# One written order of issue for every engine of a long-convolution, modulation and sparse-expert block

## The chip, the cores and the metric

The kernel runs on one core of a Trainium2 chip. The metric is the device time of the whole program in microseconds (us), as a median of several executions. The engines are TensorE (PE; PEld is its weight load), VectorE (DVE), ScalarE (ACT), GpSimd (POOL) and SyncE (SP, which here only issues DMAs). Each works through its own queue in order.

## The reference, cut to what matters

The input has 2048 tokens of 640 channels. Six modulation vectors come from c and w_mod. Part A is a long convolution over the tokens, written with FFTs; part B picks eight tokens and runs a gated MLP on them.

```python
sa, ca, ga, sb, cb, gb = (silu(c) @ w_mod) in six parts
h = layernorm(x) * (1 + ca) + sa                 # x = A_q
kv = (four-tap causal convolution of A_k) * A_v
y = irfft(rfft(pad(kv)) * rfft(pad(A_ssm_k)))[:2048] + kv * A_ssm_D
x = x + ga * (h * y)
h = layernorm(x) * (1 + cb) + sb
r = h @ w_r;  idx = the 8 tokens with the largest r
out_B = (silu(h[idx] @ w_gate) * (h[idx] @ w_up)) @ w_down * sigmoid(r[idx])
x = x + gb * (h + scatter_add(idx, out_B))
```

## The kernel before

The 640 channels are five blocks (0 to 4) of 128. Tokens are 16 groups m of 128. For each block the filter (gA) and the product kv (xA) are Fourier-transformed in two matmul stages, multiplied, and transformed back in two.

- load_kv brings k and v of a block in transposed, by DMA transposes on SP. conv applies the four taps as matmuls with diagonal matrices (make_diag), VectorE multiplies by v, and kvT goes to DRAM through POOL's queue; load_xA reads it back in another layout.
- stage_A multiplies 16 slices by the table RA, four to a PSUM tile, and each of the four tiles is evacuated into A. stage_B multiplies A by the table FT: eight PSUM tiles of 1024 columns into HX. The tables come from iotas and Sin.
- product makes the complex product on VectorE, in six operations of 1024 elements for each half of a block, with three temporaries.
- stage_BT is the first inverse stage (table IT), four tiles into U, stored to DRAM (Ud) by POOL; load_uA reads it back. stage_AT finishes the inverse (table RAT), multiplies by h, adds into xq, takes the statistics of the second layer norm (bn_stats, L398) and transposes xq to get the router's sums.
- In between stand the modulation (load_wmod, modulation), and the first layer norm: statistics (L471), then h in 16 operations (L479) and four pairs of 2560 wide ones (L483, L484).
- Tail: the statistics are aggregated (bn_aggr), xn is normalised, the eight tokens are selected by small VectorE operations and matmuls, xn is gathered by one-hot matmuls, three projections follow (L657, L677), then for every group six matmuls with the identity add up gb*sb, xq and xn*gb*(1+cb) (L693 to L695), ScalarE copies (L696), SP stores, and POOL scatter-adds the eight rows (L701).

All PSUM tiles of two banks come from one ring of four. A helper (Balance.copy, L44 and L46) gives each evacuation to ScalarE or, in a set share (0.4, then 0.2, then 0.125), to VectorE; a line L44 or L46 in the profile is that helper. The order of SP and POOL is the order of the program text; TensorE, ScalarE and VectorE are ordered by the framework's scheduler.

Of the kernel before, what the change touches and what calls it, by code (L numbers as in the profile page):

```python
# [9 lines left out]
P = 128  # L10
# [9 lines left out]
NB = 5  # L20
# [11 lines left out]
class Balance:  # L32


    def __init__(self, nc):
        self.nc = nc
        self.share = 0.0
        self.acc = 0.0

    def copy(self, out, in_):  # L40
        self.acc += self.share
        if self.acc >= 1.0 - 1e-9:
            self.acc -= 1.0
            self.nc.vector.tensor_copy(out=out, in_=in_)  # L44
        else:
            self.nc.scalar.copy(out=out, in_=in_)  # L46


def _kernel_body(ctx, tc, A_q, A_k, A_v, A_shift_k, A_ssm_k, A_ssm_D,
# [3 lines left out]
    ctx.enter_context(tc.manual_schedule(engines={mybir.EngineType.SP, mybir.EngineType.Pool}))  # L53
    bal = Balance(nc)
# [22 lines left out]
    kTs, vTs, gAs = [], [], []  # L77

    def load_kv(b):
        kT = ring.tile([P, 16 + S_TOK], BF, name="kT", tag="K")  # L80
        vT = ring.tile([P, S_TOK], BF, name="vT", tag="K")
# [3 lines left out]
        kTs.append(kT)  # L85
        vTs.append(vT)
# [16 lines left out]
    trig = big.tile([P, 4, 1024], F32, name="trig", tag="HX", bufs=3)  # L103
# [20 lines left out]
    load_kv(0)
    with nc.allow_non_contiguous_dma(reason="tiny transposed loads"):
        nc.scalar.dma_start(out=shk_bf[:], in_=A_shift_k.rearrange("(b p) j -> p b j", p=P))
        load_g(0, nc.scalar)
        Dt_rows = bass.AP(tensor=Dt[:].tensor, offset=Dt[:].offset, ap=[[16 * Dt[:].ap[0][0], 8], [1, NB * M]])
        D_rows = bass.AP(tensor=A_ssm_D.tensor, offset=A_ssm_D.offset, ap=[[1, 8], [8, NB * M]])
        nc.scalar.dma_start(out=Dt_rows, in_=D_rows)  # L130
        load_g(1, nc.scalar)
        nc.scalar.dma_start(out=cT_bf[:], in_=c.rearrange("o (t p) -> p (o t)", p=P))
        nc.scalar.dma_start(out=wr_c[:], in_=B_w_r.rearrange("(t p) -> p t", p=P))
    load_kv(1)
    V_ph = trig[:, 0:2, :]
    for hf in range(2):
        iota(trig[:, hf, :].rearrange("p (a b) -> p a b", a=8), [[4, 8], [64, P]], base=32 * hf + 1)
    nc.gpsimd.memset(halfpi[:], math.pi / 2)
    iota(irow[:], [[1, P]])
    nc.gpsimd.memset(onesb[:], 1.0)  # L140


    shk_f = const.tile([P, NB, 4], F32, name="shk_f")

    def make_diag(b):
        if b == 0:
            V.tensor_copy(out=shk_f[:], in_=shk_bf[:])
        for j in range(4):
            V.tensor_scalar(out=diag[:, b, j, :], in0=ident[:], scalar1=shk_f[:, b, j:j + 1], scalar2=None,
                            op0=ALU.mult)  # L150

    def diag_b(b):
        return diag[:, b]

    ecol = const.tile([P, 1], F32, name="ecol")
    V.tensor_scalar(out=ecol[:], in0=pidx[:], scalar1=-7.5, scalar2=1.0 / 16, op0=ALU.add, op1=ALU.mult)
    V.tensor_scalar(out=ecol[:], in0=ecol[:], scalar1=MAGIC, scalar2=None, op0=ALU.add)
    V.tensor_scalar(out=ecol[:], in0=ecol[:], scalar1=-MAGIC, scalar2=None, op0=ALU.add)
    mcol = const.tile([P, 1], F32, name="mcol")
# [36 lines left out]
    IT = const.tile([P, M, 3, P], BF, name="IT")

    def make_table(hf):
        k0 = 8 * hf
        if hf == 0:  # L200
            V.tensor_scalar(out=pc[:], in0=pidx[:], scalar1=1.0 / 8192, scalar2=None, op0=ALU.mult)
        ph, qq, ab = trig[:, hf, :], trig[:, 2, :], trig[:, 3, :]
        V.tensor_scalar(out=qq, in0=ph, scalar1=pc[:], scalar2=MAGIC, op0=ALU.mult, op1=ALU.add)
        V.tensor_scalar(out=qq, in0=qq, scalar1=-MAGIC, scalar2=None, op0=ALU.add)
        V.scalar_tensor_tensor(out=ph, in0=ph, scalar=pc[:], in1=qq, op0=ALU.mult, op1=ALU.subtract)
        fl = lambda s: FT[:, s, k0:k0 + 8, :].rearrange("p a b -> p (a b)")
        nc.scalar.activation(out=fl(1), in_=ph, func=ACT.Sin, scale=TWO_PI)
        nc.scalar.activation(out=fl(2), in_=ph, func=ACT.Sin, scale=-TWO_PI)
        V.scalar_tensor_tensor(out=ab, in0=ph, scalar=-1.0, in1=ph, op0=ALU.mult, op1=ALU.max)
        nc.scalar.activation(out=fl(0), in_=ab, func=ACT.Sin, scale=-TWO_PI, bias=halfpi[:])  # L210

    short_tables(0)
    make_diag(0)
    make_table(0)
    make_table(1)

    def make_inverse_table():
        for s, d in ((0, 1), (1, 2), (2, 0)):
# [3 lines left out]
            bal.copy(IT[:, :, d, :], pt[:])  # L222


    def stage_A(src, A, u):
        for g4 in range(4):
# [5 lines left out]
            bal.copy(o, ps[:])  # L232

    def stage_B(A, HX):
        for kk in range(8):
            ps = ps_tile([P, 2, 512])
            for i in range(2):
                k2 = 2 * kk + i
                f = lambda a: a.rearrange("p kc u d -> p (kc u d)")
# [6 lines left out]
            bal.copy(HX[:, 2 * kk:2 * kk + 2].rearrange("p k c u d -> p (k c u d)"),  # L246
                     ps[:].rearrange("p a b -> p (a b)"))

    T3 = {}

    def product(xt, ux, ht, uh):
        if "a" not in T3:
            T3["a"] = ring.tile([P, 2, 8, P], BF, name="Ta", tag="V", bufs=2)
            T3["b"] = ring.tile([P, 8, P], BF, name="Tb", tag="V", bufs=2)
        t0, t1, t2 = T3["a"][:, 0], T3["a"][:, 1], T3["b"][:]
        for hk in range(2):
            ks = slice(8 * hk, 8 * hk + 8)
            Xr, Xi = xt[:, ks, 0, ux, :], xt[:, ks, 1, ux, :]
            Hr, Hi = ht[:, ks, 0, uh, :], ht[:, ks, 1, uh, :]
# [501 lines left out]
```

## Time and profile before

| | us |
|---|---|
| median of 3 runs (range) | 274.51 (273.98 to 276.78) |
| the profiled execution's own time | 272.93 |
| its span, first to last instruction | 271.1 |
| busy: PE, DVE, ACT, POOL | 164.4, 182.0, 114.3, 15.5 |
| mean granted clock of TensorE (1 is 2.4 GHz) | 0.81 |

The profile is one execution. A busy time is the sum of an engine's instructions, which can overlap by some 0.08 us on VectorE; the chain of work gives what one instruction adds. Idle time of an engine that isn't late costs nothing.

### The profile page before, as it was taken

To read this page: it belongs to the slowest core of one execution; us is meant where nothing else is said; L and a number is where in the kernel's file an instruction comes from. 1 tells how busy PE (TensorE), PEld (TensorE's weight loads), DVE (VectorE), ACT (ScalarE), POOL (GpSimd) and SP (SyncE) were. 2 spreads that over 40 slices of the span, in tenths; PEclk is the share of its full clock that TensorE was granted. 3 is DMA by queue.
4 is the path that set the end of the run, shared out by engine and by line. 5 is a ranking of instruction groups with operands and counts; after the bars stand their busy time and mean duration, and the time that the engine had idled before them with its cause. 6 is when DMAs were issued, how large, how long until landed. Compare 5 with 4: busy or idle time off the path is not lost.

```text
span 271.1 us, 3680 instructions
## 1 busy us (share of the span) xinstructions
PE 164.4 (61%) x1428; PEld 116.6 (43%) x1428; DVE 182.0 (67%) x443; ACT 114.3 (42%) x124; POOL 15.5 (6%) x40
## 2 busy tenths in 40 slices
PE   0039969999998705650693879386455410489950
PEld 0025546557665504420372648265355400375730
DVE  5159965762477999999969219977867899502300
ACT  0149356344868703600671789135310115002850
POOL 5000200000000010000000000002100000000002
PEclk9999997999999965786588699959955755558995
DMA  8960999999999210500004400534889770000450
GB/s 152 237 76 4 245 239 243 361 378 256 251 347 244 100 77 4 155 0 0 0 9 180 123 0 7 217 92 165 299 265 392 232 248 1 2 2 0 154 210 28
DMA packets 67897, 40.64 MB, mean 150 GB/s; under 512 B 44768, under 2 KB 64680, under 8 KB 67880
## 3 DMA queue, kind: packets, MB, share of 16 engines
q1 hardware_dynamic: 58944, 31.48, 43.1%
q0 software_dynamic: 2192, 7.88, 7.6%
q10 hardware_dynamic: 6744, 1.06, 2.6%
q8 instruction: 11, 0.18, 0.3%
q14 instruction: 6, 0.05, 0.1%
HBM read 24.67 MB, written 10.50 MB: 130 GB/s over the span
## 4 chain that ended last, share of the span: by engine, by line
PE 38%; DVE 34%; DMA 10%; issue 10%; ACT 3%; POOL 1%; POOLq 1%; SPq 0%; DVEq 0%; ACTq 0%
PE ps L389 4%; DVE st L471 4%; PE ps L240 4%; PE ps L229 4%; DMA kvd<-kvT 4%; DMA gA<-in_A_ssm_k_dram 3%; DVE t L394 3%; PE ps L349 3%; PE ps L307 3%; DMA xq<-in_A_q_dram 2%; PE ps L277 2%; PE ps L677 2%; PE ps L279 2%; DVE xq L396 2%; DVE h L479 2%
## 5 line engine op out<-in xcount | busy, mean ns | idle before, releaser
L240 PE MATMUL ps<-A,FT 128*128 128x512 bf16 x80 | 33.1, 414 | 18.8 <-ACT HX L46 12.7
L46 ACT CAST HX<-ps 128x1024 bf16<-128x1024 f32 x31 | 29.9, 1023 | 32.2 <-DVE HX L263 16.9
L46 ACT CAST A<-ps 128x1024 bf16<-128x1024 f32 x30 | 28.3, 1028 | 17.9 <-PE ps L229 17.9
L229 PE MATMUL ps<-RA,gA 128*128 128x256 bf16 x80 | 14.1, 349 | 21.4 <-DVE gA L324 21.1
L242 PE MATMUL ps<-A,FT 128*128 128x256 bf16 x80 | 23.4, 293 | 0.0
L244 PE MATMUL ps<-A,FT 128*128 128x256 bf16 x80 | 23.4, 293 | 0.0
L46 ACT COPY xT<-ps 128x2048 bf16<-128x2048 bf16 x4 | 7.5, 1866 | 34.8 <-PE ps L401 34.8
L277 PE MATMUL ps<-IT,HX 128*128 128x256 bf16 x80 | 19.8, 289 | 2.5 <-DVE HX L264 2.3
L46 ACT CAST U<-ps 128x1024 bf16<-128x1024 f32 x18 | 17.4, 1020 | 8.6 <-PE ps L279 8.0
L229 PEld LDWEIGHTS <-gA 128*128 128x128 bf16 x80 | 9.7, 124 | 24.8 <-DVE gA L324 21.4
L279 PE MATMUL ps<-IT,HX 128*128 128x256 bf16 x80 | 19.4, 289 | 0.5 <-DVE HX L265 0.5
L44 DVE CAST A<-ps 128x1024 bf16<-128x1024 f32 x10 | 12.1, 1222 | 10.9 <-PE ps L229 10.9
L307 PE MATMUL ps<-kT,early 128*128 128x512 bf16 x80 | 18.1, 379 | 0.4 <-ACT A L46 0.4
L242 PEld LDWEIGHTS <-FT 128*128 128x128 bf16 x80 | 8.4, 105 | 20.1 <-issue 18.4
L394 DVE TENSOR_TENSOR t<-ps,h 128x1024 bf16<-128x1024 f32 x10 | 12.0, 1222 | 6.5 <-PE ps L389 4.0
L398 DVE BATCH_NORM_STATS2 st<-xq 128x6 f32<-128x128 bf16 x80 | 16.0, 280 | 0.1
L471 DVE BATCH_NORM_STATS2 st<-xq 128x6 f32<-128x320 bf16 x32 | 13.6, 465 | 3.3 <-DMA xq<-in_A_q_dram 3.3
L401 PE MATMUL ps<-ident,xq 128*128 128x128 bf16 x80 | 6.5, 245 | 15.2 <-DVE xq L396 15.2
L696 ACT CAST xq<-ps 128x640 bf16<-128x640 f32 x16 | 11.1, 692 | 11.0 <-PE ps L695 10.1
L309 DVE TENSOR_TENSOR kvT<-ps,vT 128x1024 bf16<-128x1024 f32 x10 | 12.2, 1222 | 4.0 <-PE ps L307 3.8
L229 PE MATMUL ps<-RA,xA 128*128 128x256 bf16 x80 | 13.2, 331 | 0.6 <-ACT A L46 0.5
L244 PEld LDWEIGHTS <-FT 128*128 128x128 bf16 x80 | 8.4, 105 | 11.2 <-issue 3.0
(189 smaller groups left out, 337.0 us busy)
## 6 DMA issues: line engine op xcount, KB each, us to landing
Ud<-U POOLq DMA_DIRECT2D x10, 512.0 KB, 2.9
uA<-Ud SPq DMA_DIRECT2D x10, 512.0 KB, 4.0
kvd<-kvT POOLq DMA_DIRECT2D x5, 512.0 KB, 5.1
xA<-kvd SPq DMA_DIRECT2D x5, 512.0 KB, 5.1
xq<-in_A_q_dram SPq DMA_DIRECT2D x4, 640.0 KB, 7.7
out_dram<-xq SPq DMA_DIRECT2D x4, 640.0 KB, 3.2
wg<-in_B_w_gate_dram SPq DMA_DIRECT2D x1, 2160.0 KB, 11.7
wu<-in_B_w_up_dram SPq DMA_DIRECT2D x1, 2160.0 KB, 16.4
```

The costliest lines, as they stand in the source:

```text
L46: self.nc.scalar.copy(out=out, in_=in_)
L229: nc.tensor.matmul(ps[:, bb // 2, :, (bb % 2) * 8:(bb % 2) * 8 + 8], lhsT=src[:, 4 * g4 + bb, :], rhs=RA[:].rearrange("p k c e -> p (k c) ...
L240: nc.tensor.matmul(ps[:, i, :], lhsT=FT[:, 0, k2, :], rhs=f(A[:, 2 * k2:2 * k2 + 2]), start=True, stop=False)
L242: nc.tensor.matmul(ps[:, i, 0:256], lhsT=FT[:, 1, k2, :], rhs=f(A[:, 2 * k2 + 1:2 * k2 + 2]), start=False, stop=False)
L244: nc.tensor.matmul(ps[:, i, 256:512], lhsT=FT[:, 2, k2, :], rhs=f(A[:, 2 * k2:2 * k2 + 1]), start=False, stop=True)
L277: nc.tensor.matmul(ps[:, i, :], lhsT=xt[:, k2, 0, ux, :], rhs=IT[:, k2, 1:3, :].rearrange("p a b -> p (a b)"), start=True, stop=False)
L279: nc.tensor.matmul(ps[:, i, :], lhsT=xt[:, k2, 1, ux, :], rhs=IT[:, k2, 0:2, :].rearrange("p a b -> p (a b)"), start=False, stop=True)
L307: nc.tensor.matmul(ps[:, i, :], lhsT=diag_b(b)[:, j, :], rhs=kT[:, n0 - j:n0 - j + 512], start=(j == 0), stop=(j == 3))
L309: V.tensor_tensor(out=kvT[:, 1024 * i2:1024 * i2 + 1024], in0=ps[:].rearrange("p a b -> p (a b)"), in1=vT[:, 1024 * i2:1024 * i2 + 1024], ...
L394: V.tensor_tensor(out=t[:].rearrange("p m (g j) -> p m g j", g=2), in0=ps[:].rearrange("p g m j -> p m g j"), in1=h[:, :, cc].rearrange("p ...
L398: V.bn_stats(out=st2[:, m, b, :], in_=xq[:, m, c0:c0 + P])
L471: V.bn_stats(out=st[:, m, hf, :], in_=xq[:, m, hf * 320:hf * 320 + 320])
```

## The change

Every queue gets its order from one text. The stages become generators that stop after each piece (an evacuation, a half of a product, four groups of statistics), and a string ORDER names the pieces in the order in which all engines get them; a star sends an evacuation to VectorE, the others go to ScalarE. The functions keep their contents but for these points:

- The product works in place in HX, in two operations of 2048 (filter broadcast over the real and imaginary rows) and two of 1024 per half; filter and kv of one block now share one HX, and HX has two buffers in place of three.
- The diagonals of blocks 1 to 4 and the constants of the selection are made on POOL; the absolute value of the table is made on ScalarE; kv is stored by SP from a single kvT buffer; the first loads come in another order, and the tiny loads of D move to SP.
- bn_aggr is replaced by eight short operations over all groups (moments).
- In the tail the PSUM ring is released and split. Two matmul pairs per group add gb*sb and xq ("base", two PSUM tiles), in portions put before the gather, between the projections, before and after the last one; VectorE then multiplies and adds xn ("finish"), and SP stores xn.

```diff
+ORDER = """
+START RA DIAG0 DIAG2 TAB0 LK2 RA TAB0:2 C0:2 LK1 G0 TAB1:3 DIAG1 G0* C2:2 G0 LXA0 G0* RAT:2 C1 LW:4 IT DIAG3
+IT IT* C1 MOD LG2 X0* X0 X0* X0 MOD LW:2 B0* B0 B0* B0 P0 B0:4 LG1 P0:2 MOD:4 OG LXA1 G1:3 G2 P0 COL LX G1
+X1:2 BT0 X1 Sx G2 Sx:8 BT0 LK3 C3 X1 BT0:2 LXA2 B1:4 Sx:2 G2:2 LG3 B1 Sx:5 X2 LK4 Sx C3 X2:2 LG4 X2 B1:2 P1
+H:2 B1 B2:3 G3 P1:2 DIAG4 C4 G3 B2 H B2 G3 P1 G3 LXA3 X3 H:3 B2:3 C4 LXA4 H:3 X3:3 BT1:3 H BT1 B3:5 LU0 H G4
+B3 P2 G4 B3 H B3 P2:2 AT0 X4 AT0 G4:2 BT2:2 LU1 WG P2 P3 X4:2 S0 P3 X4 BT2 AT1 BT2 B4:2 P3 LU2 B4:3 P3 P4 B4:3
+BT3:2 S0 P4:2 S0 BT3:2 LU3 P4 AT1 S0 S1 BT4 S1:2 BT4:3 S1 R0 AT2:2 R0 R1 S2:3 AT3:2 R1 S2 S3:2 R2 LU4 AT4 R2
+R3 AT4 R3 R4 WG S3:2 S4:4 R4 WD TC
+"""
-    ctx.enter_context(tc.manual_schedule(engines={mybir.EngineType.SP, mybir.EngineType.Pool}))
+    ctx.enter_context(tc.manual_schedule())
...
+            (V if b == 0 else nc.gpsimd).tensor_scalar(out=dg[:, j, :], in0=ident[:], scalar1=shk_f[:, b, j:j + 1],
...
+        kvT = ring.tile([P, S_TOK], BF, name="kvT", tag="V")
...
+        nc.sync.dma_start(out=kvds[b][:], in_=kvT[:])
...
-            V.tensor_tensor(out=t0, in0=Xr, in1=Hr, op=ALU.mult)
-            V.tensor_tensor(out=t1, in0=Xi, in1=Hi, op=ALU.mult)
-            V.tensor_tensor(out=t2, in0=Xr, in1=Hi, op=ALU.mult)
-            V.tensor_tensor(out=Xi, in0=Xi, in1=Hr, op=ALU.mult)
-            V.tensor_tensor(out=Xr, in0=t0, in1=t1, op=ALU.subtract)
-            V.tensor_tensor(out=Xi, in0=Xi, in1=t2, op=ALU.add)
+            X = hx[:, ks, :, 1, :]
+            Xr, Xi = hx[:, ks, 0, 1, :], hx[:, ks, 1, 1, :]
+            Hr, Hi = (hx[:, ks, i:i + 1, 0, :].to_broadcast([P, 8, 2, P]) for i in range(2))
+            V.tensor_tensor(out=T2[:], in0=X, in1=Hi, op=ALU.mult)
+            V.tensor_tensor(out=X, in0=X, in1=Hr, op=ALU.mult)
+            yield
+            V.tensor_tensor(out=Xr, in0=Xr, in1=T2[:, :, 1, :], op=ALU.subtract)
+            V.tensor_tensor(out=Xi, in0=Xi, in1=T2[:, :, 0, :], op=ALU.add)
+            yield
...
+    def t_S1():
         for m in range(M):
+            for hf in range(2):
+                V.bn_stats(out=st1[:, m, hf, :], in_=xq[:, m, hf * 320:hf * 320 + 320])
+            yield
+        mu1, var1 = moments(st1[:], 4, 160, "a")
...
+    def base(ms):
+        for m in ms:
+            po = back.tile([P, 2, 512], F32, name="po", tag="o", bufs=2)
+            for hf in range(2):
+                cc = slice(hf * 320, hf * 320 + 320)
+                nc.tensor.matmul(po[:, hf, 0:320], lhsT=ident[:], rhs=gbs[:, cc], start=True, stop=False)
+                nc.tensor.matmul(po[:, hf, 0:320], lhsT=ident[:], rhs=xq[:, m, cc], start=False, stop=True)
+            nc.scalar.copy(out=xq[:, m, :].rearrange("p (h d) -> p h d", h=2), in_=po[:, :, 0:320])
...
+    norm(rest[4:])
+    base(range(0, 4))
...
+    def finish(ms, store=None):
+        for m2 in ms:
+            x2 = xn[m2 // 4][:, 2 * (m2 % 4):2 * (m2 % 4) + 2, :]
+            V.tensor_tensor(out=x2, in0=x2, in1=gbo[:, None, :].to_broadcast([P, 2, D]), op=ALU.mult)
+            V.tensor_tensor(out=x2, in0=x2, in1=xq[:, 2 * m2:2 * m2 + 2, :], op=ALU.add)
+            if m2 % 2 == 1:
+                nc.sync.dma_start(out=out_d[:, 2 * m2 - 2:2 * m2 + 2, :],
+                                  in_=xn[m2 // 4][:, 2 * (m2 % 4) - 2:2 * (m2 % 4) + 2, :])
...
     pg = proj(wg)
...
+    base(range(4, 8))
     pu = proj(wu)
...
+    finish(range(0, 2))
+    hT = small.tile([P, NFC, NSEL], BF, name="hT")
+    V.tensor_tensor(out=hT[:], in0=gs[:], in1=pu[:], op=ALU.mult)
+    base(range(8, 10))
...
+    base(range(10, 16))
+    finish(range(2, 4))
```

The names in ORDER: C convolution halves, G and X stage_A for filter and kv, B stage_B, P product, BT and AT the inverse stages, S statistics and R router sums of a block, Sx and H the first layer norm, MOD, OG, COL modulation, TAB, RA, RAT, IT tables, LK, LG, LXA, LU, LW, LX, WG, WD loads of k and v, filter, kv, inverse data, w_mod, x and the expert weights, TC the selection's constants. "P0:2" is two pieces of block 0's product. Rings that held four buffers (K for k, v, U, t and xT; G for gA, xA and uA) get five and six.

## Rows read from the trace of the kernel before

**Rows 1.** Windows: busy us (instructions) per engine, granted clock, DMA share, GB/s.
```profile
18.00:36.00 18.00, 17.23 (x98) 10.39 (x99) 17.84 (x42) 13.46 (x14) 1.57 (x4) 1.00 0.56 126
36.00:69.00 33.00, 29.89 (x191) 19.25 (x190) 17.71 (x23) 15.77 (x19) 1.18 (x3) 0.95 1.09 293
69.00:90.00 21.00, 18.63 (x158) 13.19 (x157) 14.88 (x25) 16.75 (x17) 0.53 (x1) 1.00 1.02 268
90.00:105.00 15.00, 3.40 (x32) 2.45 (x29) 15.00 (x58) 3.51 (x4) 1.28 (x3) 0.72 0.17 70
105.00:131.00 26.00, 11.54 (x58) 7.52 (x59) 25.66 (x47) 7.25 (x8) 0.00 (x0) 0.70 0.14 41
158.00:183.00 25.00, 19.11 (x173) 14.83 (x173) 18.38 (x39) 13.44 (x14) 1.06 (x2) 0.86 0.26 86
248.20:262.00 13.80, 13.18 (x97) 9.28 (x96) 4.17 (x5) 10.96 (x16) 0.00 (x0) 1.00 0.41 144
```

**Rows 2.** Waits: who waited for whom, us in total, times, longest.
```profile
ACT HX L46 <- DVE HX L263: 16.9, 1, 16.9
```

**Rows 3.** Chain that ended last, middle of the kernel: start us, us, what.
```profile
57.24 3.46 PE ps L307 x16
...
87.67 0.60 DVE Ta L260
...
94.64 0.75 DVE st L471 x2
...
111.55 5.70 DVE h L479 x16
117.25 2.80 DVE h L483 x2
...
143.22 2.35 DVE t L394 x2
...
208.84 3.45 PE ps L389 x32
```

**Rows 4.** The same chain, the tail.
```profile
214.78 3.19 DVE st L398 x16
...
223.50 3.92 DVE xn L591 x11
...
237.70 3.89 PE ps L657 x140
...
242.01 6.22 PE ps L677 x28
...
262.13 3.24 DMA out_dram<-xq
```

**Rows 5.** Timeline of ScalarE near 70 us: start us, us, engine, line, operation.
```profile
69.82 5.59 ACT L46 CAST A<-ps 128x1024 bf16<-128x1024 f32 x6 [0.24 <-PE ps L229]
```

**Rows 6.** Timeline of the first 5 us, POOL and VectorE.
```profile
1.82 0.29 POOL masks.py:199 TENSOR_SCALAR_AFFINE_SELECT ident<-ident 128x128 bf16<-128x128 bf16 x1
...
2.26 1.99 POOL L117 IOTA trig<- 128x1024 f32 x2
...
3.47 0.86 DVE L157 TENSOR_SCALAR ecol<-ecol 128x1 f32<-128x1 f32 x1
...
4.39 0.15 DVE L158 TENSOR_SCALAR ecol<-ecol 128x1 f32<-128x1 f32 x1
```

**Rows 7.** Timeline of SP, which issues transposes and loads.
```profile
25.70 1.24 SPq L83 DMA_TRANSPOSE kT<-in_A_k_dram  x1
...
55.93 10.73 SPq L83 DMA_TRANSPOSE kT<-in_A_k_dram  x1
```

**Rows 8.** DMA issues: count, KB each, median us to landing.
```profile
xA<-kvd SPq DMA_DIRECT2D x5, 512.0 KB, 5.1
xq<-in_A_q_dram SPq DMA_DIRECT2D x4, 640.0 KB, 7.7
...
early<-in_w_mod_dram SPq DMA_DIRECT2D x2, 800.0 KB, 7.5
```

More of the change, by code (lines that the diff above doesn't have):

```diff
@@ L231, in stage_A, with t_G, t_X, t_C @@
             o = A[:, :, u, g4 * 32:g4 * 32 + 32].rearrange("p kc (g j) -> p g kc j", g=2)
-            bal.copy(o, ps[:])
-    def stage_B(A, HX):
+            evac(o, ps[:])
+            yield
+    def t_G(b):
+        V.tensor_tensor(out=gAs[b][:, :, 0], in0=gAs[b][:, :, 0], in1=Dt[:, b * M:(b + 1) * M], op=ALU.add)
+        yield from stage_A(gAs[b], b, 0)
+    def t_X(b):
+        yield from stage_A(xAs[b], b, 1)
+    def t_C(b):
+        kT, vT = kTs[b], vTs[b]
+        kvT = ring.tile([P, S_TOK], BF, name="kvT", tag="V")
+        for i2 in range(2):
+            ps = ps_tile([P, 2, 512])
+            for i in range(2):
+                n0 = 16 + 512 * (2 * i2 + i)
+                for j in range(4):
+                    nc.tensor.matmul(ps[:, i, :], lhsT=diags[b][:, j, :], rhs=kT[:, n0 - j:n0 - j + 512],
+                                     start=(j == 0), stop=(j == 3))
+            V.tensor_tensor(out=kvT[:, 1024 * i2:1024 * i2 + 1024], in0=ps[:].rearrange("p a b -> p (a b)"),
+                            in1=vT[:, 1024 * i2:1024 * i2 + 1024], op=ALU.mult)
+            if i2 == 0:
+                yield
+        kvds[b] = dram.tile([P, S_TOK], BF, name="kvd%d" % b)
+        nc.sync.dma_start(out=kvds[b][:], in_=kvT[:])
+        yield
+    def t_B(b):
+        A = As[b]
+        HX = HXs[b] = big.tile([P, M, 2, 2, P], BF, name="HX", tag="HX", bufs=2)
+        f = lambda a: a.rearrange("p kc u d -> p (kc u d)")
         for kk in range(8):
@@ L315, in _kernel_body @@
[L315 to L329 removed]
+        yield
+    h_ = {}
+    rsum = small.tile([P, M, 2], F32, name="rsum")
@@ new lines, in t_S, with t_R @@
+    def t_S(b):
+        if b == 0:
+            h_["st2"] = small.tile([P, M, NB, 6], F32, name="st2", tag="st")
+        st2 = h_["st2"]
+        for m in range(M):
+            V.bn_stats(out=st2[:, m, b, :], in_=xq[:, m, b * P:(b + 1) * P])
+            if m % 4 == 3:
+                yield
+    def t_R(b):
+        pt = ps_tile([P, M, P], BF)
+        for m in range(M):
+            nc.tensor.transpose(pt[:, m, :], xq[:, m, b * P:(b + 1) * P], ident[:])
+        xT = ring.tile([P, M, P], BF, name="xT", tag="K", bufs=5)
+        evac(xT[:], pt[:])
+        yield
+        pr = ps_tile([P, M, 2])
+        for m in range(M):
+            nc.tensor.matmul(pr[:, m, :], lhsT=xT[:, m, :], rhs=wcol[:, b, :], start=True, stop=True)
+        if b == 0:
+            V.tensor_copy(out=rsum[:], in_=pr[:, :, :])
+        else:
+            V.tensor_tensor(out=rsum[:], in0=rsum[:], in1=pr[:, :, :], op=ALU.add)
+        yield
@@ L459, in _kernel_body @@
-    bal.share = 0.125
-    product(X1, 1, X0, 0)
-    stage_B(A2, X2)
-    stage_BT(X1, 1, 0)
-    load_uA(0)
-    og, sg = modv[:, 1, :], modv[:, 0, :]
-    V.tensor_tensor(out=og, in0=og, in1=modv[:, 2, :], op=ALU.mult)
-    V.tensor_tensor(out=sg, in0=sg, in1=modv[:, 2, :], op=ALU.mult)
-    st = small.tile([P, M, 2, 6], F32, name="st1", tag="st")
-    mv1 = small.tile([P, M, 2], F32, name="mv1")
-    for m in range(M):
-        for hf in range(2):
-            V.bn_stats(out=st[:, m, hf, :], in_=xq[:, m, hf * 320:hf * 320 + 320])
-        V.bn_aggr(out=mv1[:, m, :], in_=st[:, m, :, :])
@@ new lines, in _kernel_body, with once, run @@
+    tasks = {}
+    def once(f, b):
+        f(b)
+        yield
+    def run(name, n):
+        kind = name.rstrip("0123456789")
+        if name not in tasks:
+            arg = name[len(kind):]
+            tasks[name] = MAKERS[kind](*([int(arg)] if arg else []))
+        for _ in range(n):
+            next(tasks[name])
+    MAKERS = dict(START=t_START, TC=t_TC, RA=lambda: short_tables(0), RAT=lambda: short_tables(2), DIAG=t_DIAG,
+                  TAB=t_TAB, IT=t_IT, G=t_G, X=t_X, C=t_C, B=t_B, P=t_P, BT=t_BT, LU=t_LU, AT=t_AT, S=t_S, R=t_R,
+                  LW=t_LW, MOD=t_MOD, OG=t_OG, COL=t_COL, LX=t_LX, Sx=t_S1, H=t_H, WG=t_WG, WD=t_WD,
+                  LK=lambda b: once(load_kv, b), LG=lambda b: once(load_g, b), LXA=lambda b: once(load_xA, b))
@@ new lines, in _kernel_body, with pm_tile @@
+    for item in ORDER.split():
+        name, _, n = item.partition(":")
+        evac.vector = name.endswith("*")
+        run(name.rstrip("*"), int(n) if n else 1)
+    for name, t in tasks.items():
+        assert next(t, "end") == "end", name
+    front.close()
+    back = ctx.enter_context(tc.tile_pool(name="back", bufs=1, space=bass.MemoryType.PSUM))
+    wg, wu, wd = W["g"], W["u"], W["d"]
+    def pm_tile(shape, dtype=F32):
+        return back.tile(list(shape), dtype, name="pm", tag="m", bufs=2)
@@ L594, in _kernel_body, with norm @@
-    prT = ps_tile([M, P], BF)
+    xn = [big.tile([P, 8, D], BF, name="xn", tag="HX", bufs=2) for _ in range(2)]
+    on_act = NORM_ON_SCALAR
+    def norm(ms):
+        for m in ms:
+            o, i_ = xn[m // 8][:, m % 8, :], xq[:, m, :]
+            if m in on_act:
+                nc.scalar.activation(out=o, in_=i_, func=ACT.Identity, scale=rs2[:, m:m + 1], bias=nm2[:, m:m + 1])
+            else:
+                V.tensor_scalar(out=o, in0=i_, scalar1=rs2[:, m:m + 1], scalar2=nm2[:, m:m + 1], op0=ALU.mult,
+                                op1=ALU.add)
@@ L595, in _kernel_body @@
+    rest = [m for m in range(M) if m not in on_act]
+    norm(on_act)
+    prT = pm_tile([M, P], BF)
     nc.tensor.transpose(prT[:, :], r_bf[:], ident[:])
+    norm(rest[0:1])
     rT = small.tile([M, P], F32, name="rT")
```

626 lines of the change are left out of this document (265 added, 361 removed).

## Prediction

> **What bounds the kernel now.** I read the windows first. From 36 to 90 us TensorE is busy about nine tenths of the time and the DMA is saturated, at 268 to 293 GB/s [rows 1]. From 90 to 131 us VectorE alone is full (15.0 of 15 us, 25.7 of 26), while TensorE works 3.4 and 11.5 us and ScalarE 3.5 and 7.3 [rows 1]. The list of waits says why: ScalarE once waited 16.9 us to write HX until VectorE had read the old HX in the product [rows 2]; that product stood in VectorE's queue behind the layer norm's statistics (0.75 us a token group) and all of h (5.70 us, then four pairs of about 2.80) [rows 3]. So no engine bounds this kernel: long runs on one engine's queue starve the others. From 131 us on the engines take turns as well (19.1 and 18.4 of 25 us) [rows 1]. At the end lies a serial tail: after the last statistics (214.78 + 3.19 = 217.97 us) [rows 4] come selection, experts, the 96 combining matmuls, the store and the scatter-add, 53.1 us to the span's end.
>
> **Unit costs.** 16 matmuls of 512 columns take 3.46 us, 0.42 us per 1000 columns; 32 of 128 took 3.45 us late in the kernel, 0.84 per 1000, which is the 1.2 GHz level [rows 3]. VectorE takes 0.60 us for a bf16 operation 1024 wide and 1.40 for 2560, so 0.07 + 0.52 per 1000 elements; from PSUM 1024 cost 1.17 (2.35 for two) [rows 3]. ScalarE evacuates 1024 in 0.93 us when it doesn't wait (5.59 for six) [rows 5].
>
> **Product.** A half of a block was six operations of 1024, 3.60 us; it becomes two of 2048 (1.13 each, by the line above) and two of 1024: 3.46. The elements are the same, so ten halves save 1.4 us in all. [...]
>
> **Moves between engines.** Seven evacuations stay on VectorE (the starred names in ORDER) and ScalarE takes the others, at 0.93 us where VectorE pays 1.17. VectorE also loses 16 diagonals, two absolute values and the bn_aggr. The moves count in the stage sums below. The 16 diagonals and the eight table operations go to POOL, and this isn't free: a one-element VectorE operation that takes 0.15 us took 0.86 beside POOL's iotas, and ended as these did (2.26 + 1.99 = 4.25 us) [rows 6]. A POOL operation of 128x128 is 0.29 us [rows 6], so 24 of them can hold VectorE 0 to 7 us, more if they are slower than that row; I take 2, since they are spread and VectorE gives some up anyway. [...]
>
> **Stage A, up to block 3's first convolution half.** The matmul head starts earlier: the first Sin no longer stands behind a wait for c. But the DMA decides this stage. SP's order puts block 3's transposes behind all of w_mod and x, and a transpose issued onto a full queue held SP 10.73 us [rows 7]. Before, the queue paused until block 2's load went out at 25.70 [rows 7]; now that load follows block 0's at once, so I let the queue run on from 18 us, when the first four transposes are through. After that it must move four transposes, three kv stores, two kv loads and two filter blocks (11 x 512 KB), six of w_mod (800 KB) and four of x (640 KB) [rows 8]: 13.0 thousand KB or 13.3 MB, at 293 to 268 GB/s 45.4 to 49.6 us. So block 3's v lands at 63 to 68 us; I take 66. The stores of kv move from POOL's queue to SP's, behind transposes, and kvT has one buffer, so VectorE waits in its queue for each store, with layer norm and product behind it; this costs nothing in the sum, as VectorE, by the same count of pieces as in stage B, has some 41 us of work in these 66. If that cover is gone it costs up to 5 us for each of three stores (a transfer of that size in [rows 8]).
>
> **Stage B, the rest of ORDER's line 3 to the end of line 7.** I count each line's pieces and take the fullest engine. Line 3: 16 evacuations, ScalarE 14.9 us (VectorE 12.9). Line 4: 27 evacuations, 25.1 (VectorE 22.9, TensorE 22.8). Line 5: VectorE 23.6 (nine product pieces of P2, P3 and P4's first are 16.1, three inverse halves AT at 1.17 + 0.60 make 5.3, h 1.4, statistics 0.8). Line 6: VectorE 26.5 (P4 4.7, six AT halves 10.6, 13 quarter blocks of statistics at 0.80 = 10.4, rest 0.8). Line 7: VectorE 6.9. Sum 97.0 us; VectorE alone has 92.8, TensorE 75 by its columns at 2.4 GHz. Nothing runs without waits across a four-deep PSUM ring: the fullest engine reached 0.91, 0.89 and 0.76 in three mixed stretches, and 0.99 where one engine starved the others [rows 1]. I take 0.90: 107.8 us, with 97 to 129 as ends. What is late next is ScalarE in line 4, VectorE in 5 and 6.
>
> **Tail.** Four products of 1280 leave the selection's chain (0.73 each by the unit cost, 2.9), one of 11 normalisations moves to ScalarE (0.36, a share of 3.92 [rows 4]), and eight short operations replace the 16 aggregations that stand between 217.97 and the first normalisation at 223.50 [rows 4] (5.5 us with the inverse root; I take 0.5 of it, at most 2): -3.8 us. The 16 matmuls (5120 columns) now between the two projections delay the second by up to 4.3 us at 1.2 GHz, the level that this stretch had (6.22 us for 28 x 320 columns [rows 4]). Then hT stands on VectorE behind the sigmoid, which waits for ScalarE's copies, and four operations of 0.73: 3.5 us against 1.95 for a projection (half of 3.89 [rows 4]): +1.6. After the experts' last matmul the old tail took 13.9 us to the last copy (248.23 to 262.13 [rows 4]; 96 matmuls at 2.4 GHz [rows 1]); now 24 matmuls and six copies (0.69 each, 10.96 for 16 [rows 1]) run beside VectorE's delta (640 from PSUM, about 0.8 by the 1.17 for 1024) and eight operations of 0.73, 6.6 together: -7.3. The store (3.24 us [rows 4]) and the scatter behind it stay. Sum -5.2: 47.9 us; 44 if the interleaved matmuls lift the clock to 2.4 GHz before the experts, 51 if the delta waits.
>
> **Sum.** 66 + 107.8 + 2 + 47.9 = 223.7 us of span. The profiled execution of before lay 1.8 us above its span and 1.6 below the median: 227.1 us.
>
> **Rivals.** *Ring-bound:* fixed orders make the engines wait for each other as in the stretch at 0.76 [rows 1]; stage B takes 129 us, the kernel 248. For it: four PSUM slots as before, and no queue can now step past a late piece. Against: the pieces alternate. *Smooth:* stage B at 97 us, POOL costs nothing, DMA at its upper rate: 212. For it: VectorE ran at 0.99 whenever its inputs were there. [...] *Slower than before:* TensorE stays at 1.2 GHz from its start to the tail, because small pieces with gaps replace its long runs. Its work there is some 262 thousand columns, 110 us at 2.4 GHz and 220 at 1.2 [rows 3], longer than any other queue. With a start at 11 us (an estimate: it was fully busy from 18 [rows 1], less the wait for c) that gives 11 + 220 + 51 + 3.4 = 285. It decides once the mean granted share in that stretch is below about 0.52 (110 of the 212 us that a time of 277 leaves). For it: the clock was 0.72 and 0.70 where VectorE starved TensorE; against: 0.95 to 1.00 with full queues, 0.86 in the mixed stretch [rows 1], and TensorE would have no gap left at the low level.
>
> **How the numbers follow.** Forecast 0.55, ring-bound 0.19, smooth 0.13, broadcast 0.05, low clock 0.05; 0.03 for a ring so tight (0.6) that nothing is gained. The range, 208 to 248, takes in forecast, broadcast, nearly all of smooth and half of ring-bound. Within 1% is about what a measurement of this kernel can tell from no change; faster by more holds all but the last two cases, 0.92.
>
> **What would show it.** Stage A: VectorE's first multiplication of block 3's taps by v starts near 66 us, with the DMA row full until then. Stage B: no VectorE run of h longer than three operations, TensorE and ScalarE busy about 0.7 each, last statistics near 176 us. Product: 2048-wide operations near 1.2 us. Tail: 48 us, with copies of x between the projections. The prediction is wrong if one queue stands over 10 us in stage B on one late transfer, if the granted clock there is near 0.5, or if the tail's matmuls delay the experts by more than the 4.3 us.

## The result and the profile after

The changed kernel takes 212.98 us (median of 4 runs, 211.63 to 214.55), the kernel before 274.42 beside it: ratio 0.7745, 95% interval 0.7692 to 0.7798, 61.4 us less. The forecast was 227.1 with a range of 208 to 248. The time is that of the *smooth* rival (212), which had been given a chance of 0.13.

From the page of the changed kernel; each digit is the busy share of a fortieth of the span, in tenths:

```profile
span 211.5 us, 3596 instructions
PE 152.4 (72%) x1388; PEld 107.4 (51%) x1398; DVE 167.1 (79%) x368; ACT 131.8 (62%) x144; POOL 27.5 (13%) x59
PE   0659849997849998999978998675831069979600
DVE  7769844696858999999999999999999891092930
ACT  0568745678857998999999998563221562520700
DMA  7999999999999939004979955677939000015060
```

Its windows (columns as in [rows 1]):

```profile
18.00:36.00 18.00, 14.02 (x108) 9.27 (x109) 12.17 (x17) 11.84 (x13) 2.50 (x5) 0.91 1.09 315
36.00:56.00 20.00, 17.95 (x136) 13.13 (x136) 14.87 (x31) 14.94 (x18) 0.00 (x0) 0.97 1.05 288
56.00:64.00 8.00, 5.27 (x30) 3.31 (x30) 5.19 (x14) 5.01 (x6) 0.93 (x2) 0.87 1.20 247
64.00:100.00 36.00, 34.15 (x241) 23.68 (x244) 34.80 (x68) 34.50 (x38) 3.67 (x8) 1.00 0.57 132
100.00:140.00 40.00, 34.35 (x342) 27.00 (x343) 39.10 (x70) 34.85 (x37) 4.39 (x9) 1.00 0.81 267
140.00:161.00 21.00, 11.64 (x190) 10.40 (x187) 20.80 (x66) 7.46 (x4) 3.60 (x9) 0.83 0.71 236
```

The DMA row is full up to 74 us, so all through the stage that ends at 64. From there to the last statistics VectorE is busy 34.80 + 39.10 + 20.80 = 94.7 of 97 us, and TensorE and ScalarE work beside it at 0.86 to 0.96 until 140. The stretches of [rows 1] in which VectorE alone was full and TensorE worked less than half the time are gone; 140 to 161 us comes nearest, with TensorE at 11.64 of 21. The last statistics end at 161.0 us; before it was 218.0 [rows 4]. So 57 of the 60 us of span were won ahead of the tail, and the tail gave 2 to 3.

The end of the head, as a timeline (start, us, engine, what; in brackets the idle time before it and what ended it):

```profile
59.43 0.39 PE L288 MATMUL ps<-kT,dg 128*128 128x512 bf16 x1
60.13 1.04 ACT L57 CAST U<-ps 128x1024 bf16<-128x1024 f32 x1
61.50 0.80 POOL L346 DMA_DIRECT2D Ud<-U  x1 [39.56 <-ACT U L57]
62.31 0.13 POOL L94 MEMSET kT<- 128x16 bf16 x1
62.49 1.67 PE L288 MATMUL ps<-kT,dg 128*128 128x512 bf16 x6 [2.67 <-POOL kT L94]
64.20 1.23 DVE L290 TENSOR_TENSOR kvT<-ps,vT 128x1024 bf16<-128x1024 f32 x1 [3.01 <-PE ps L288]
```

Block 3's convolution started at 59.43, when kT had landed, and then stood 2.67 us for the memset of kT's padding. That was ready to run, but behind U's store in GpSimd's queue, and the store waited for ScalarE's evacuation. VectorE's 3.0 us behind it are the only wait that the list of waits has for VectorE from 64 us to the last statistics at 161 us; before 64 it has others, the longest of 4.2 us.

The tail, likewise:

```profile
177.92 2.01 PE L700 MATMUL pm<-xsT,wg 128*128 128x8 bf16 x70 [0.52 <-DVE xsT L694]
184.01 1.96 PE L700 MATMUL pm<-xsT,wu 128*128 128x8 bf16 x70
184.84 0.20 ACT L722 ACTIVATE sig<-inf 8x1 f32<-8x1 f32 x1
185.07 0.14 DVE L723 TENSOR_SCALAR sig<-sig 8x1 f32<-8x1 f32 x1 [7.14 <-ACT sig L722]
188.31 0.26 DVE L726 TENSOR_TENSOR hT<-gs,pm 128x112 bf16<-128x112 bf16 x1
188.63 6.88 PE L731 MATMUL py<-wd,hT 128*8 128x320 bf16 x28 [1.56 <-DVE hT L726]
202.26 0.83 DVE L709 TENSOR_TENSOR xn<-xn,xq 128x1280 bf16<-128x1280 bf16 x1
```

Four base tiles lie between the projections (179.8 to 184.0). The sigmoid is queued behind their four copies on ScalarE, and VectorE, which has finish(0:2) ready behind it, waits 7.14 us.

### The profile page after: what moved, and what is told of

Same layout as the page of the kernel before. It is cut to its first block, busy times and chain, and to the rows that moved or that the text cites. A ratio compares the mean times of both kernels' runs of the same rounds, so it can differ in the third digit from the quotient of the medians.

```text
span 211.5 us, 3596 instructions
## 1 busy us (share of the span) xinstructions
PE 152.4 (72%) x1388; PEld 107.4 (51%) x1398; DVE 167.1 (79%) x368; ACT 131.8 (62%) x144; POOL 27.5 (13%) x59
## 4 chain that ended last, share of the span: by engine, by line
DVE 47%; issue 23%; PE 15%; DMA 6%; ACT 3%; POOL 2%; POOLq 1%; SPq 1%; DVEq 0%
DVE st L390 6%; DMA vT<-in_A_v_dram 5%; DVE t L380 4%; DVE T L324 3%; PE py L731 3%; ACT HX L57 3%; DVE kvT L290 3%; DVE h L539 3%; DVE h L535 3%; DVE h L541 3%; DVE st L524 3%; PE ps L288 2%; DVE HX L325 2%; DVE xn L709 2%; DVE xn L708 2%
## 5 line engine op out<-in xcount | busy, mean ns | idle before, releaser
L57 ACT CAST A<-ps 128x1024 bf16<-128x1024 f32 x36 | 36.1, 1080 | 7.9 <-PE ps L267 7.8
L57 ACT CAST HX<-ps 128x1024 bf16<-128x1024 f32 x38 | 37.0, 1119 | 1.8 <-PE ps L310 1.8
L288 PE MATMUL ps<-kT,dg 128*128 128x512 bf16 x77 | 20.2, 403 | 10.9 <-DMA kT<-in_A_k_dram 7.1
L629 ACT CAST xq<-po 128x640 bf16<-128x640 f32 x16 | 10.6, 693 | 14.5 <-PE po L628 12.8
L288 PEld LDWEIGHTS <-dg 128*128 128x128 bf16 x80 | 8.0, 102 | 20.5 <-DVE dg L229 7.0
L375 PE MATMUL ps<-RAT,uA 128*128 128x128 bf16 x160 | 11.3, 228 | 3.9 <-DVE t L380 3.4
L324 DVE TENSOR_TENSOR T<-HX 128x2048 bf16<-128x2048 bf16 x10 | 12.2, 1222 | 1.3 <-ACT HX L57 0.7
L375 PEld LDWEIGHTS <-uA 128*128 128x128 bf16 x160 | 10.3, 103 | 4.6 <-DMA uA<-Ud 2.4
L310 PEld LDWEIGHTS <-FT 128*128 128x128 bf16 x80 | 7.8, 98 | 9.4
L325 DVE TENSOR_TENSOR HX<-HX 128x2048 bf16<-128x2048 bf16 x10 | 12.2, 1225 | 0.4
```

Source lines behind the costliest of these rows:

```text
L288: nc.tensor.matmul(ps[:, i, :], lhsT=diags[b][:, j, :], rhs=kT[:, n0 - j:n0 - j + 512], start=(j == 0), stop=(j == 3))
L310: nc.tensor.matmul(ps[:, i, 256:512], lhsT=FT[:, 2, k2, :], rhs=f(A[:, 2 * k2:2 * k2 + 1]), start=False, stop=True)
L324: V.tensor_tensor(out=T2[:], in0=X, in1=Hi, op=ALU.mult)
L375: nc.tensor.matmul(o, lhsT=uA[:, bb, cs * P:(cs + 1) * P], rhs=RAT[:, cs, :].rearrange("p (m e) -> p m e", e=8), start=(cs == 0), stop=(cs ...
```

## The experiments

Times are medians with the kernel before beside them; it took 274.7 to 275.8. "Stage B" is the stretch from block 3's first multiplication to the last router sum: 64.2 to 161.1, 96.9 us, in the changed kernel.

**1. The order written, but not enforced.** `manual_schedule()` becomes `manual_schedule(engines={SP, Pool})`.

> The text of the changed kernel as it is, but with TensorE, ScalarE and VectorE left to the scheduler that ordered them in the kernel before; SyncE and GpSimd keep the written order. Theory (the gain is in the sequence of the pieces, whoever hands it to the engines): the scheduler follows the sequence of the text where nothing holds it, so TensorE's list stays as it is up to the tail, and the time stays at 211 to 218 us. Rival 1 (the gain is in the explicit order itself, which keeps the scheduler from choosing otherwise): it goes back by tens of microseconds, to 240 to 275 us.

Measured 208.25 us, ratio 0.758 (0.750 to 0.766): faster than the changed kernel. The scheduler spoils the head and mends the tail. Block 3's first multiplication comes at 70.2: VectorE's queue now starts with casts that wait for tiny loads.

```profile
DVE wrf L458 <- DMA wr_c<-in_B_w_r_dram: 7.8, 1, 7.8
DVE shk_f L226 <- DMA shk_bf<-in_A_shift_k_dram: 3.1, 1, 3.1
```

The last router sum is at 162.8 all the same, and the tail takes 42.7 us in place of 50.4; VectorE's wait for the sigmoid is 0.4. So it is not the fixing of the order that gives the gain: with the text's sequence left in place, the scheduler does as well.

**2. Whole stages.** The generators of each block run whole at the place of their last piece: "... LG3 LK4 Sx:17 C3:2 LG4 X2:4 B1:8 DIAG4 P1:4 G3:4 LXA3 B2:8 C4:2 LXA4 X3:4 BT1:4 LU0 H:12 B3:8 ...".

> Everything of the changed kernel except the interleaving: each stage of a block (G, X, C, B, P, BT, AT, S, R, H and the first statistics) is issued whole, at the place where its last piece stood. Same operations, same engines, same buffers, still one written order. Theory (pieces side by side keep VectorE from waiting while ScalarE empties a stage's PSUM, and the other way round): the stretch from the first multiplication of block 3 to the last statistics, 96.8 us in the changed kernel, grows by 20 to 50 us, because 12 pieces of h (18 us of VectorE) and 17 of statistics stand in one run beside nothing of ScalarE; time 233 to 263 us. Rival 2 (the gain is in wider operations, moves between engines and more buffers): within 5 us of 213.

Measured 239.52 us, ratio 0.868 (0.858 to 0.879): 26.5 us of the 61 are lost. The time lies in the theory's band, but stage B grew by 16 us only, less than the 20 that the theory had as its least; the head, of which it said nothing, grew by 11. What the trace shows in stage B is sharper than the theory:

```profile
90.15 0.22 DVE L272 TENSOR_TENSOR gA<-gA,Dt 128x16 bf16<-128x16 bf16 x1
90.43 3.59 PE L265 MATMUL ps<-RA,gA 128*128 128x256 bf16 x16 [5.95 <-DVE gA L272]
103.83 1.23 DVE L288 TENSOR_TENSOR kvT<-ps,vT 128x1024 bf16<-128x1024 f32 x1 [13.46 <-PE ps L286]
```
```profile
90.00:106.00 16.00, 15.47 (x84) 9.67 (x87) 2.04 (x4) 11.29 (x13) 0.00 (x0) 0.81 0.01 1
```

The addition of D into gA, 0.22 us long, stood behind the whole product of block 1 on VectorE's queue and held TensorE 5.95 us. TensorE then went through all of G3 and B2 before C4, and held VectorE 13.46: from 90 to 106 us VectorE worked 2.0. The same addition for block 4, behind all of h and the first inverse stage, held TensorE 8.3 us.

**3. Whole stages in the old sequence.** ORDER as in 2, but x, its statistics and h behind the second block's forward transform, and AT2 to AT4 last: "... B1:8 LX LK4 C3:2 ... P0:4 BT0:4 LU0 G2:4 X2:4 B2:8 OG Sx:17 COL H:12 G3:4 ... BT4:4 LU4 AT2:2 S2:4 R2:2 AT3:2 ...".

> The changed kernel's operations, engines, buffers and tail, with its stages issued whole and in about the sequence of the kernel before: x is loaded and its statistics and h are made behind the second forward transform, and the last three AT stages stand at the end. It asks where the rest of the gain is that the run with whole stages in the new sequence did not give back (that one took 239.5 us, 27 of the 61). Theory (what came when: a late x, and the loads for block 3 and 4 late): most of it is sequence: 258 to 275 us. Rival (moves of work between engines, wider operations and more buffers gave the rest): within 5 us of 239.5.

Measured 284.25 us, ratio 1.035 (1.026 to 1.044): slower than the kernel before, and above the theory's range.

Waits and a window from block 3 on:

```profile
DVE t L378 <- PE ps L373: 20.3, 5, 11.3
DVE kvT L288 <- PE ps L286: 19.1, 2, 18.6
DVE kvT L288 <- DMA kvd<-kvT: 3.5, 1, 3.5
```
```profile
105.00:150.00 45.00, 20.79 (x138) 14.64 (x138) 38.64 (x86) 21.44 (x24) 0.00 (x0) 0.73 0.10 29
```

The picture of [rows 1] is back: 45 us with VectorE at 0.86 and the others at half or less. The wait of 18.6 us, from 63 to 82, was for block 3's first convolution, whose k SP issued at 72.4, behind w_mod and x. So without the new order the new operations, engines and buffers don't show a gain. How much they gave is open, as this sequence is near the old one, not the same, and the scheduler had improved on the old one. From 284 the sequence of the stages and their loads gives 45 us, the interleaving of the pieces 26.5; this split is for this reconstruction. The new order with the old operations and rings was not run.

**4. Half-width product.** Each 2048 wide operation is cut in two.

```diff
-            V.tensor_tensor(out=T2[:], in0=X, in1=Hi, op=ALU.mult)
+            for i in range(2):
+                V.tensor_tensor(out=T2[:, :, i, :], in0=X[:, :, i, :], in1=Hi[:, :, i, :], op=ALU.mult)
...
```

> Only the product's 2048 wide multiplications are cut into two of 1024 each (20 operations more, still in place; 16 of the 20 stand in the stretch that VectorE fills). A 1024 wide operation of the same kind takes 0.68 us there and a 2048 wide one 1.22, so each cut costs 0.15 us. Theory (VectorE sets the time of that stretch): 20 x 0.15 = 3 us more at most, about 2.4 of them on the path: 215 to 216 us. Rival 2 (wide operations are a main part of the gain): 5 us or more. Rival 3 (PSUM buffers or TensorE set that stretch, VectorE has room): no change, within 1 us.

Measured 211.14 us, ratio 0.766 (0.759 to 0.773): no loss. Stage B takes 96.9 us as before. It lies with the rival that VectorE has room, but for another reason: my price was wrong, as a listed duration holds a part that overlaps the neighbour: in the changed kernel two 1024 wide operations listed at 0.69 and 0.68 us start 0.61 apart (123.95 and 124.56 us). By busy time 16 halves of one operation cost 10.3 us against 9.8 for eight wide ones, 1.0 us for both in stage B, which the run can't tell from nothing. So this run doesn't decide who bounds stage B; the next does.

**5. More for VectorE.** B4's eight evacuations get a star.

> The eight evacuations of block 4's forward transform go from ScalarE to VectorE (B4 starred); they stand at about 118 to 135 us, where VectorE is busy 39 of 40 us and ScalarE has some slack. On VectorE one took 1.224 us in the head. Theory (VectorE sets this stretch, with no room): 8 x 1.22 = 9.8 us more: 221 to 224 us. Rival (TensorE with ScalarE's evacuations sets it and VectorE is only busy beside it): ScalarE's eight go away, so no change or a gain: 209 to 214 us.

Measured 221.53 us, ratio 0.810 (0.803 to 0.816): 8.5 us more; the last router sum is 9.4 us later (0.7 of it lost before stage B). From 118 to 140 us ScalarE's work is only 5.4 us and VectorE is full:

```profile
118.00:140.00 22.00, 15.17 (x107) 10.21 (x107) 21.83 (x30) 5.44 (x6) 1.59 (x3) 0.92 0.38 130
```

What VectorE gets it pays for nearly one to one. It bounds this stretch.

**6. Less for VectorE.** AT's result goes through ScalarE to bf16.

```diff
-            V.tensor_tensor(out=t[:].rearrange("p m (g j) -> p m g j", g=2), in0=ps[:].rearrange("p g m j -> p m g j"),
-                            in1=h[:, :, cc].rearrange("p m (g j) -> p m g j", g=2), op=ALU.mult)
+            evac(t[:].rearrange("p m (g j) -> p m g j", g=2), ps[:].rearrange("p g m j -> p m g j"))
+            yield
+            V.tensor_tensor(out=t[:], in0=t[:], in1=h[:, :, cc], op=ALU.mult)
```

> In the last stage (AT) the result in PSUM is first copied to bf16 by ScalarE, one piece ahead, and VectorE then multiplies it from SBUF. VectorE's multiplication out of PSUM takes 1.21 us; a 1024 wide one on bf16 takes 0.69 (the addition behind it, same tiles): ten of them. ScalarE gets ten copies of about 1.1 us, at 111 to 160 us, where it is busy 7.5 of the last 21 us. Theory (VectorE sets the time of this stretch alone): 10 x 0.52 = 5.2 us less, up to 1 us of it lost where VectorE waits for a copy: 208 to 209 us. Rival (ScalarE and TensorE are as full, or the copy's delay is not covered): 212 to 216 us.

Measured 212.58 us, ratio 0.775 (0.769 to 0.782): nothing; the rival. VectorE's multiplications did fall to 0.69 us each, but the last router sum is at 162.0:

```profile
100.00:111.00 11.00, 9.63 (x89) 7.04 (x89) 10.76 (x13) 11.00 (x14) 0.14 (x1) 1.00 0.89 279
111.00:120.00 9.00, 7.99 (x71) 6.08 (x70) 7.71 (x14) 9.00 (x12) 0.91 (x2) 1.00 0.93 344
120.00:130.00 10.00, 10.00 (x87) 7.53 (x85) 9.58 (x15) 10.00 (x13) 0.68 (x2) 1.00 0.53 160
```
```profile
DVE rsum L408 <- PE ps L404: 2.8, 3, 2.2
DVE t L382 <- ACT t L57: 2.4, 4, 1.1
```

VectorE waited 5.2 us for copies and router sums, just what it had saved. ScalarE was full from 100 to 130 us (30.0 of 30; 29.2 in the changed kernel), where the first three copies came, but only 1.1 us of the waits lies there. At the first router sum VectorE was even 2.9 us ahead of the changed kernel (140.9 against 143.8). It lost this and more behind it, where ScalarE was busy 12.6 of 22 us (139 to 161); the chain that ended last goes there through block 4's U, its store, its reading back and the inverse stage. TensorE's granted clock was 0.67 from 140 to 150 us, where the changed kernel had 1.00, and 16 of its matmuls there took 1.89 us in place of 1.05:

```profile
137.14 7.42 DMA Ud<-U
144.69 4.14 DMA uA<-Ud
148.87 1.89 PE ps L375 x16
```

By this chain, with 5 us less on VectorE the end of stage B is set by the last U's way through DRAM and back, and by the transposes behind it.

**7. Three PSUM buffers** in place of four.

> Three PSUM buffers instead of four ahead of the tail, everything else as in the changed kernel. Theory (VectorE's own work sets the stretch after the first multiplication of block 3; TensorE is ahead of it, in the changed kernel VectorE waits there 3.0 us in all, at its start): one buffer less takes away lead, but 1 to 6 us show: 214 to 219 us. Rival (the ring of buffers is what the stages run against, as in the forecast's case of 248 us): 20 us or more: above 232 us.

Measured 214.06 us, ratio 0.779 (0.773 to 0.786): 1 us. Stage B takes 98.2 us. The *ring-bound* rival falls with it: the fourth slot is hardly needed.

**8. Padding first.** "Sx:8 BT0 LK3 C3" becomes "Sx:8 LK3 BT0 C3".

> In the written order LK3 stands ahead of the second piece of BT0 instead of behind it, so GpSimd clears the padding of block 3's kT before it issues the store of U and not after it. Theory (the end of the head was set by GpSimd's queue: TensorE waited 2.7 us for that memset with kT already landing, and VectorE 3.0 us for the convolution behind it): block 3's first multiplication comes 2.5 to 3 us earlier than 64.2, and everything behind it too: 210 to 211 us. Rival (the loads set it, the memset only came last by a little): 0 to 1 us: 212 to 213 us.

Measured 209.96 us, ratio 0.766 (0.762 to 0.771). Block 3's first multiplication starts at 61.7, 2.5 us earlier; VectorE's wait there is now 0.5 us, for the load of vT. Stage B keeps its 97.0 us. The theory holds, and the loads alone would have ended the head at 61.7.

**9. The old order of the tail.** All base tiles after the last projection, finish(0:2) behind hT.

> Only the tail is taken apart again: all sixteen base tiles come after the last projection, and finish(0:2) no longer stands ahead of hT. By the terms of the prediction the experts start 3.8 us and end 4.3 and about 3 us earlier, and sixteen base tiles of 1.07 us follow them instead of six: 17.2 against 6.4. The sum is 10.8 - 11.1 = about zero: 211 to 216 us. Rival (the interleaved tail is worth the 7.3 us that were counted for it alone): 218 to 221 us. Second rival (the interleaving costs more than it gives, as the 7.1 us wait of VectorE for the sigmoid hints): 205 to 210 us.

Measured 213.21 us, ratio 0.778 (0.769 to 0.787): no difference; the tail is 49.3 us long. The interleaving of the tail gave nothing.

**10. A tail by VectorE's waits.** x is no longer overwritten by the bases, so that five tiles need not wait for the normalisation; six bases go to VectorE (vbase: xq += gbs); ScalarE's sigmoid moves ahead of the projections (not shown) and VectorE's operation on it behind hT:

```diff
+    base(range(0, 5))
     mu, var = moments(h_["st2"][:], 2 * NB, D // (2 * NB), "b")
...
-            nc.scalar.copy(out=xq[:, m, :].rearrange("p (h d) -> p h d", h=2), in_=po[:, :, 0:320])
+            nc.scalar.copy(out=xb[m // 2][:, m % 2, :].rearrange("p (h d) -> p h d", h=2), in_=po[:, :, 0:320])
...
+    base(range(8, 10))
     pu = proj(wu)
+    vbase(12, 4)
+    vbase(10, 2)
+    finish(range(0, 1))
     hT = small.tile([P, NFC, NSEL], BF, name="hT")
```

> The tail alone is rewritten. Base tiles 0 to 9 go into free buffers instead of over x, so that five of them can run on TensorE and ScalarE while VectorE still works on the statistics; bases 10 to 15 are two additions on VectorE (2560 and 1280 wide, by the 1.49 us of h's addition about 2.3 us), made while it waits for the experts; the sigmoid is no longer in front of finish and hT; the last projection follows hT at once. Theory (in the changed kernel's tail of 50.5 us, VectorE idles 7.1 us behind the sigmoid and TensorE's base tiles stand in front of each projection at half clock): gather at 172 to 173 instead of 175.2, hT at 179 to 182 instead of 188.3, last finish at 188 to 191 instead of 203.1, and the end 10 to 14 us earlier: 199 to 203 us. Rival (the tail is set by the stores and the low clock of TensorE whatever the order): 208 to 213 us.

Measured 205.47 us, ratio 0.748 (0.743 to 0.754): 7.5 us where the theory had 10 to 14, the tail 41.9. hT came at 183.8, late: VectorE waited 2.0 us for the gather and 2.4 for the second projection, ahead of which I had left bases 8 and 9.

**11. Together**: 6, 8 and 10, the last with vbase moved into the wait for the gather and bases 8 and 9 behind the second projection.

> Together: the padding of block 3 ahead of U's store, AT's copies on ScalarE, and the rewritten tail with two repairs: the additions of bases 10 to 15 stand in VectorE's wait for the gather (2.0 us there), and bases 8 and 9 come behind the second projection (TensorE was 2.4 us late with it). Theory (these lie one behind the other on one path, so that their gains add): 3.0 + 4.5 + 7.5 + 3.5 = 18.5 us less than 213.0: 193 to 197 us. Rival (one of them only moves the wait, for example to ScalarE, whose copies of AT would then delay the forward transforms): 200 to 205 us.

Measured 199.58 us, ratio 0.728 (0.721 to 0.734): between the two, next to the rival's band. The tail shrank to 38.3 us and the padding gave its part; 6 made stage B 0.8 us longer (97.8 against 97.0 in 8), as it did alone.

**12. Together, with 6 for blocks 2 to 4 alone.** `if b < 2:` keeps VectorE's multiplication from PSUM; a block's two copies are issued ahead, with statistics between ("AT2:2 S1 R0 AT2 S1 AT2").

> As the run with everything together (199.6 us), but AT's copies on ScalarE are kept for blocks 2 to 4 alone, which stand at 140 to 160 us, where ScalarE was busy 7.5 of 21 us; blocks 0 and 1 go back to VectorE. The copies of a block are issued together, with two to four pieces of statistics between them and the multiplications. Theory (the ten copies gained nothing because four of them came where ScalarE was itself full, 10.0 of 10 us from 120 to 130, and the others came too short before their use): without them the padding and the tail alone give 213.0 - 3.0 - 12.1 = 197.9 us, the six copies take 6 x 0.52 = 3.1 us more: 194.5 to 196.5 us. Rival (the chain of one AT to the next, with transposes and rsum, sets the last 20 us, whatever VectorE has to do): 197.5 to 200 us.

Measured 197.96 us, ratio 0.721 (0.717 to 0.725), 15 us under the changed kernel. Stage B takes 95.5 us (61.8 to 157.3) against 97.0 in 8: 1.5 us of the 3.1.

```profile
DVE rsum L417 <- PE ps L413: 1.1, 2, 0.8
DVE kvT L290 <- DMA vT<-in_A_v_dram: 1.0, 1, 1.0
DVE t L391 <- ACT t L57: 0.3, 1, 0.3
```
```profile
141.22 5.35 DMA uA<-Ud
```

The time lies in the rival's band. In stage B VectorE waits 1.4 us, where in 8 it didn't wait at all (the 1.0 for vT lies just ahead of the stage). The chain that ended last goes, as in 6, through the reading back of block 4's U (last row, from that chain) and through the transposes; in 8 it stays on VectorE there.

## Why the prediction was right, and where it was off

- **The cause** that the prediction gave, long runs on one engine's queue starving the others, is shown by 2 and 3: the same operations in whole stages take 240 and 284 us. That the order is enforced is no part of it (1). The range held the time; the single forecast was 14 us too long.
- **Stage A**, 66 us forecast, 64.2 measured. The last wait was not the one forecast: the prediction looked at SP's queue and the loads, and it was GpSimd's queue (8). It had counted what GpSimd's operations may cost VectorE, not what waits in GpSimd's own queue. The loads were done at 61.7 (8), ahead of the forecast's 63 to 68: from 18 us to there the DMA of the changed kernel moved some 12.9 MB at a mean of 295 GB/s, about the upper of the forecast's two rates, and the forecast had counted 13.3 MB. That 64.2 is so near 66 is thus partly luck.
- **Stage B**, 107.8 forecast, 96.9 measured, is the term that was mis-sized, by nearly the whole error. The line sums of 97.0 stand; the division by 0.90 doesn't. The shares that it came from (0.91, 0.89, 0.76 [rows 1]) were stretches of a kernel whose queues starved each other, so they carry what the change removes; and [rows 1] had a mixed stretch against them, 18 to 36 us, with VectorE at 0.99 and TensorE at 0.96. Run 5 shows VectorE without room. That the line sums hit 96.9 is partly luck. ScalarE took about 0.98 us for an evacuation (31.3 us for 32 into HX), not 0.93, which would make lines 3 and 4 longer; but VectorE was busy 94.7 us of the 97 (its own pieces had been counted at 92.8), so that it is VectorE's work over all lines that adds up, and not the fullest engine of each.
- **POOL**, 2 us forecast, none seen in stage B. Nine statistics took 3.62 us beside block 4's diagonals and 3.62 without them (67.31 and 57.57 us in the timeline). They read one SBUF input; no VectorE operation with two stood beside those diagonals, so for such the run shows nothing there.
- **kvT's single buffer** cost nothing, as forecast; where the cover was gone (3), two stores held VectorE 3.4 and 3.5 us.
- **Product**, 1.4 us to be saved: nothing is to be seen. A 2048 wide operation takes 1.22 us, not 1.13; from the start of one half to the next (121.44 and 125.35 us) are 3.9 us, where the forecast had 3.46 and the old six operations 3.60. Cutting the wide operations costs nothing that the run shows (4). The broadcast operand runs at the rate that the forecast took, 0.52 us per 1000 elements: 1.22 us for 2048 against 0.68 for 1024 is 0.53 us per 1000 elements, and the halves of run 4, which have no broadcast, take as long as other 1024 wide ones (0.69). The case that the forecast calls broadcast, with a chance of 0.05, was that these wide operations run at half that rate; no run shows it.
- **Tail**, 47.9 forecast, 50.4 measured. From the last statistics to the gather it won 2.6 us in place of 3.8, since four bases stand in front of the gather (without them, in 9, it ends 1.1 us earlier). From the gather to the last projection it lost 6.2 (5.9 forecast), and behind the projection it won 6.9 (7.3). The projection itself was 0.7 longer. In 9 the experts' last projection starts at 181.1 and not at 188.6: the bases and what waits behind them delay it by 7.5 us. The prediction had named a delay of more than 4.3 by the matmuls as a sign of being wrong; between the projections they took 4.2, and with the 1.1 in front of the gather they are over it. The interleaving by itself gives nothing (9).

The sum: -1.8 for stage A, -10.9 for B, -2 for POOL, +2.5 for the tail make -12.2; 223.7 - 12.2 = 211.5, the span. The forecast of the time added 3.4 us to its span; here it is 1.5, as the profiled execution lay 0.3 us above the median and not 1.6 below.

## What to carry to other kernels

Where one engine's queue alternates with idle neighbours, count each engine's work and divide by no efficiency that was measured in the starved kernel: with pieces of about a microsecond side by side the fullest engine ran at 0.98. Look for small operations (a 16-column addition, a memset, a sigmoid) that stand in an in-order queue behind something that waits; here each held a whole engine for 2.7 to 8.3 us. Before taking work off the fullest engine, look at what it would wait for next: here 5 us less on VectorE met the last U's store, reading back and transposes and gave nothing (6), 3 us less gave 1.5 (12), while the first wait of stage B and the tail gave 3.0 and 7.5 (8, 10).

## What was unexpected in the hardware's behaviour

A 128x128 multiplication on GpSimd takes 0.59 us in a run of four (2.36 us for block 4's diagonals), where the affine select of the same size took 0.29 [rows 6]. In the first microseconds each of the two engines was slower beside the other than later: a 256 wide fp32 operation of VectorE took 1.03 us beside GpSimd's iota and the same line for the second table, at 22.3 us with GpSimd idle, 0.29; and block 2's diagonals took GpSimd 4.22 us while VectorE worked on diagonals and fp32 tables, those of blocks 1 and 3 2.35 us beside VectorE's operations from PSUM. What makes the difference, the trace doesn't show.

From 161 to 171 us, with TensorE busy 0.6 of 10 us, its granted clock was 0.50, and it was 0.69 and 0.67 in the windows 171 to 180 and 180 to 190, in which TensorE was busy over eight tenths. The 320 wide matmuls of the first bases begin at 0.47 us each and end at 0.30, those between the projections take 0.47 again. At 0.47 they start 0.27 us apart and at 0.30 0.14, which is 0.83 and 0.42 us per 1000 columns: the two rates of [rows 3]. The prediction and the table of the time before call them 1.2 and 2.4 GHz; the traces give the clock as a share of full speed only.
